# Sixteen early score tiles: mask and maximum as products on TensorE, the exponential in the fetch

## The chip, the core and the metric

The kernel runs on one core of one Trainium2 chip. The core has five engines that run on their own and wait for each other by semaphores: TensorE (PE in the trace, with its weight loads as PEld), VectorE (DVE), ScalarE (ACT), GpSimd (POOL) and SyncE (SP, which issues most DMAs). The metric is the device time of one execution in microseconds.

## The reference, cut to what matters

The program computes attention in which every row keeps only its 32 largest scores, and then feeds the result to a mixture of experts. There are 8 batches of 8 heads, 576 positions, and 64 values per head; the experts are 8 of 512 x 1024 and 1024 x 512.

```python
scores = scale * np.matmul(q, k.transpose(0, 1, 3, 2))
kth = np.partition(scores, -top_k, axis=-1)[..., -top_k:-top_k + 1]
scores = np.where(scores >= kth, scores, -1000000000.0)
attn = np.exp(scores - np.max(scores, axis=-1, keepdims=True))
attn = attn / (np.sum(attn, axis=-1, keepdims=True) + 1e-09)
x = np.matmul(attn, v)            # per head; then (4608, 512)
...
e_idx = np.argmax(x @ w_gate + modality_bias[modality_id], axis=1)
for e in range(E):
    h = np.maximum(x[mask] @ w1[e], 0.0)
    out[mask] = gate_w[mask, None] * (h @ w2[e])
```

## The kernel before

Scores are worked on in tiles of 128 rows by 576 columns. Two heads form a pair and have 9 tiles: eight full ones, four to a head, and one that joins the last 64 rows of both. There are 32 pairs and 288 tiles. `role(i)` is the place of tile `i` in its pair; roles 0 to 7 are the full tiles in couples (the two heads of one row block), role 8 is the joint one.

The schedule is written by hand. One pass of the main loop, a step, issues one piece of work for each of some ten tiles in different states; the engines then run their own queues in exactly that order. In step `i` the tiles are these:

- tile i+2: scores on TensorE (`qk`), copied to SBUF by ScalarE as `Ssb` (`sevac`)
- tiles i and i-1, VectorE: the maxima of six column blocks (`subs`, tile `cand`), and from them the 24 largest of a row (`chain`, tile `mg`, three maxima at L407 to L409). The third of these maxima releases `n` on GpSimd (`below`, L421), which holds the 24th largest
- tile i-3, ScalarE: `sign`, which marks and counts the scores not above that bound (tile `K`); tile i-4, GpSimd: `pool_y`, the product `y` of scores and marks (L434); tile i-5, VectorE: `find`, the next eight of a row from `y` (L438)
- in every third step three small VectorE instructions for three tiles at once, `pick` (`eq`, `jk`, `kth`, L445 to L447), which choose the 32nd largest of a row, `kth`, and on GpSimd `small` (`sm`, L415), the negated row maxima
- tile i-7, at the end of VectorE's step: the masking, in one of two forms. The usual form is `keep` (L458): ScalarE has already taken the exponential (`expo`, tile `ex`), and one VectorE instruction compares, multiplies and sums the row into `den`. GpSimd then runs a tiny `gate` (`spare`, L481) that waits for `keep`, ahead of the next `y`. The other form is for early tiles, those below tile 48 whose number is not 2 modulo 3: VectorE writes only the mask as a large negative number (`hide`, L465, tile `hT`, lent from the experts), GpSimd adds it to the scores one step later (`hidden`, L471, tile `ex`), and ScalarE takes the exponential with the row's sum (`masked`, L477, tile `P`)
- tile i-9: TensorE transposes `P` in blocks of 128 columns (`trans`), ScalarE copies the result to `PT` (`evac`), and the products with v follow (`av`)

VectorE's order inside a step comes from `arrange`, which places the pieces by a table of costs and earliest starts. The order on GpSimd is that of the calls: `hidden`, then `gate`, `pool_y`, in one step of nine two copies `qbd` (`fill`), then `below` and `small`.

Experts start when the first batch of four pairs has been routed. From then on each step also gets expert work for TensorE from a budget fixed in the program. Until then idle steps carry filler products with ones (`keep_warm`, L973). At the end, `bounds` and `beyond` check that the thresholds lay in a safe range; otherwise the program repeats the work in a slow form (`slow`).

Of the kernel before, what the change touches and what calls it, by code (L numbers as in the profile page):

```python
# [42 lines left out]
LR = LT + 2  # L43
# [13 lines left out]
QO = 0  # L57
# [20 lines left out]
def kernel(  # L78
# [274 lines left out]

    st0 = wk.tile([128, 2, 2, S], FR, name="ks", bufs=2)
    role = lambda i: (i - 1) % 9

    def unstacked(j):

# [26 lines left out]
        T[i] = {"ps": ps[:, :, :288]}  # L385

    def sevac(i):
        T[i]["S"] = sb = wk.tile([128, S], FT, name="Ssb", bufs=LR + 1 + QL - QO)
        A.activation(sb.rearrange("p (a b) -> p a b", a=2), T[i]["ps"], AF.Copy, scale=0.125)  # L389

    bnd = [(x * S) // NSUB for x in range(NSUB + 1)]
# [17 lines left out]
                lambda: V.max(m[:, 16:24], c3)]  # L409

    def small(i0):
        s = wk.tile([128, 3], FT, name="sm", bufs=6)
        for x in range(3):
            T[i0 + x]["s"] = s
        G.tensor_scalar(s, T[i0]["mg"][:, :, 0], -1.0, 1.0, op0=OP.mult, op1=OP.mult)  # L415

    def below(i):
        t = T[i]
# [68 lines left out]

    def trans(i):
        c, h = divmod(role(i), 2)
        T[i]["pt"] = psT.tile([128, 5, 128], FT, name="T")  # L490
        for x in range(4 if c < 4 and h == 0 else 5):
            PE.transpose(T[i]["pt"][:, x, :], (Pm if c == 4 else Pb[c % 2])[:, h * 512 + x * 128:h * 512 + x * 128 + 128], idf)  # L492

    def evac(i):
        c, h = divmod(role(i), 2)
        if c < 4:
            o, n = PT[:, c, 4 * h:4 + 5 * h], 4 + h
        else:
            o, n = PT[:, 1, 4:], 5
        A.activation(o, T[i]["pt"][:, :n], AF.Copy)  # L500

    def av(p, j, x):

# [469 lines left out]
            PE.matmul(ps[:, :256].rearrange("p (a b) -> p a b", a=2), onesb, onesb[:, None, :].to_broadcast([128, 2, 128]), start=True, stop=True)  # L973

    keep_warm(KW)
    bd_ = const.tile([128, 4], FT, name="bad")
    badi = const.tile([1, 1], I32, name="badi")

    def bounds():

        bt = wk.tile([128, S], BF, name="K", bufs=KB).bitcast(FT)[:, :NT]
        V.tensor_scalar(bt, kth, KTH_MIN, 0.0, op0=OP.is_le, op1=OP.add, accum_out=bd_[:, 0:1])
        V.tensor_scalar(bt, kth, KTH_MAX, 0.0, op0=OP.is_ge, op1=OP.add, accum_out=bd_[:, 1:2])

    def beyond():

        bb = bd_.bitcast(BF)[:, 4:6]
        V.tensor_scalar(bb, bd_[:, 0:2], 0.0, None, op0=OP.is_gt)
        pbad = psX.tile([128, 2], FT, name="X")
        PE.matmul(pbad, onesb, bb, start=True, stop=True)  # L990
        V.tensor_reduce(bd_[:, 3:4], pbad, axis=AX.X, op=OP.add)
        V.tensor_copy(badi, bd_[0:1, 3:4])
# [130 lines left out]
    for i in range(LAST):  # L1123
# [104 lines left out]
        if ok(u) and role(u) in (3, 7, 8):  # L1228
# [261 lines left out]
```

## Time and profile before

| what | value |
|---|---|
| time, median of 3 runs (lowest to highest) | 1192.18 us (1190.52 to 1195.83) |
| the profiled execution, its own time | 1191.36 us |
| its span (first to last instruction) | 1189.7 us |
| busy share of the span: PE, DVE, ACT, POOL | 97%, 92%, 83%, 56% |
| granted clock of TensorE, mean | 0.995 |
| first tile's `find` on VectorE | 18.6 us |
| first expert product's weights (w1b) requested | 173.97 us |

The span is the part of the time that the trace shows; what lies around it is 1.7 us here. A busy share counts every moment in which an instruction of the engine is under way; VectorE's instructions overlap at their ends, so their durations add up to more than the busy time, and the distance from one start to the next is the better measure of what one costs. TensorE's busy share before 170 us holds the fillers. The last 190 us have little attention work, and TensorE is the engine with the most to do there.

### The profile page before, as it was taken

How to read it: one execution, taken by the hardware profiler on the slowest of the kernel's cores; microseconds unless marked ns; L12 is line 12 of the kernel's file. 1: busy time of each engine (PE TensorE's matmuls, PEld its weight loads, DVE VectorE, ACT ScalarE, POOL GpSimd, SP SyncE). 2: the span in 40 equal slices, each digit the busy share in tenths (PEclk: the TensorE clock that was granted, in tenths of full speed). 3: DMA queues.
4: the chain of work that ended last, by engine and by line, in shares of the span. 5: the costliest groups of instructions: out<-in, count | busy, mean ns of one | idle time of the engine just before them, and what ended most of it. 6: DMA issues, size and time to landing. Idle time of an engine off the chain costs nothing.

```text
span 1189.7 us, 28032 instructions
## 1 busy us (share of the span) xinstructions
PE 1150.4 (97%) x7902; PEld 904.1 (76%) x7902; DVE 1089.2 (92%) x5474; ACT 981.5 (83%) x2015; POOL 670.6 (56%) x1256
## 2 busy tenths in 40 slices
PE   8889979999999999999999999999999999999998
PEld 6667768777777868777686877778687777589987
DVE  7999999999999999999999899999999999476762
ACT  5999979998889979998999899989999887355653
POOL 6888875555656565566566566557655665221111
PEclk9999999999999999999999999999999999999999
DMA  5663357653677368654785448664765554287750
GB/s 125 161 183 90 89 164 221 191 151 87 169 221 199 86 178 241 170 151 129 199 244 156 129 134 242 168 163 133 204 185 134 173 145 148 71 288 250 245 191 22
DMA packets 204323, 197.09 MB, mean 166 GB/s; under 512 B 104413, under 2 KB 151533, under 8 KB 204160
## 3 DMA queue, kind: packets, MB, share of 16 engines
q1 hardware_dynamic: 196880, 175.92, 53.4%
q0 software_dynamic: 6080, 19.00, 4.4%
q8 instruction: 66, 1.08, 0.4%
q14 instruction: 97, 0.79, 0.2%
q10 hardware_dynamic: 1200, 0.30, 0.1%
HBM read 118.63 MB, written 24.23 MB: 120 GB/s over the span
## 4 chain that ended last, share of the span: by engine, by line
PE 64%; DVE 23%; ACT 6%; issue 2%; DMA 2%; POOL 1%; SPq 0%; POOLq 0%; ACTq 0%; DVEq 0%
PE E L798 11%; PE E L811 11%; PE X L520 10%; PE S L384 8%; PE T L492 7%; DVE cand L396 6%; PE X L1085 5%; PE X L1069 4%; DVE mg L438 4%; DVE P L458 4%; PE E L1069 1%; PE X L318 1%; ACT K L428 1%; ACT Ssb L389 1%; DVE cand L407 1%
## 5 line engine op out<-in xcount | busy, mean ns | idle before, releaser
L396 DVE MAX8 cand<-Ssb 128x8 f32<-128x96 f32 x1728 | 389.5, 245 | 2.1 <-ACT Ssb L389 2.1
L434 POOL TENSOR_TENSOR y<-Ssb,K 128x576 f32<-128x576 f32 x288 | 368.2, 1279 | 8.9 <-ACT K L428 8.6
L428 ACT ACTIVATE K<-Ssb,n 128x576 bf16<-128x576 f32 x288 | 230.0, 799 | 9.2 <-POOL y L434 9.0
L384 PE MATMUL S<-ks,qs 128*128 128x288 f32 x992 | 222.7, 346 | 9.9 <-ACT Ssb L389 6.5
L389 ACT ACTIVATE Ssb<-S 128x576 f32<-128x576 f32 x284 | 187.9, 662 | 53.5 <-PE S L384 32.4
L438 DVE MAX8 mg<-y 128x8 f32<-128x576 f32 x288 | 213.4, 741 | 3.9 <-POOL y L434 3.9
L798 PE MATMUL E<-xgT,w1b 128*128 128x256 f32 x832 | 201.2, 384 | 3.5 <-ACT hT L802 1.6
L452 ACT ACTIVATE ex<-Ssb,sm 128x576 f32<-128x576 f32 x256 | 202.9, 793 | 0.0
L500 ACT ACTIVATE PT<-T 128x640 f32<-128x640 f32 (+1 forms) x288 | 193.6, 672 | 6.7 <-PE T L492 6.6
L811 PE MATMUL E<-w2b,hT 128*128 128x512 f32 x416 | 195.8, 597 | 0.5 <-ACT hT L802 0.2
L384 PEld LDWEIGHTS S<-ks,qs 128*128 128x128 f32 x992 | 152.9, 190 | 56.8 <-issue 26.0
L458 DVE SCALAR_TENSOR_TENSOR P<-Ssb,kth,ex 128x576 f32<-128x576 f32 x230 | 191.3, 832 | 3.0 <-ACT ex L452 1.7
L492 PE MATMUL T<-idf,P 128*128 128x128 f32 x1152 | 169.6, 274 | 6.3 <-ACT P L477 5.3
L798 PEld LDWEIGHTS E<-xgT,w1b 128*128 128x128 f32 x832 | 150.8, 190 | 30.0 <-ACT hT L802 6.6
L481 POOL TENSOR_SCALAR spare<-P 1x1 f32<-1x1 f32 x230 | 41.9, 182 | 211.7 <-DVE mg L407 175.0
L492 PEld LDWEIGHTS T<-idf,P 128*128 128x128 f32 x1152 | 137.6, 141 | 12.5 <-ACT P L477 8.8
L520 PE MATMUL X<-PT,vm 128*64 128x256 f32 (+1 forms) x1536 | 145.2, 331 | 1.0 <-ACT xgT L757 0.5
L520 PEld LDWEIGHTS X<-PT,vm 128*64 128x64 f32 x1536 | 87.7, 137 | 45.3 <-issue 10.7
L421 POOL TENSOR_SCALAR n<-mg 128x1 f32<-128x1 f32 x288 | 67.5, 234 | 96.4 <-DVE mg L409 78.9
L811 PEld LDWEIGHTS E<-w2b,hT 128*128 128x128 f32 x416 | 72.6, 190 | 59.6 <-issue 54.7
L428 ACT ACTIVATION_READ_ACCUMULATOR K<-Ssb,n 128x1 f32 x288 | 64.0, 222 | 0.0
L1091 POOL DMA_INDIRECT out_dram<-ot,tk x12 | 12.3, 1026 | 91.0 <-ACT ot L1090 91.0
(223 smaller groups left out, 2146.5 us busy)
## 6 DMA issues: line engine op xcount, KB each, us to landing
w1b<-in_moe_w_dram SPq DMA_DIRECT2D x76, 512.0 KB
w2b<-in_moe_w_dram SPq DMA_DIRECT2D x76, 512.0 KB
ks<-st SPq DMA_DIRECT2D x62, 288.0 KB
ks<-st SPq DMA_DIRECT2D x62, 256.0 KB
qs<-st SPq DMA_DIRECT2D x124, 128.0 KB
xg<-xs SPq DMA_DIRECT2D x19, 516.0 KB
vm<-in_v_dram SPq DMA_DIRECT2D x32, 256.0 KB
km<-in_k_dram SPq DMA_DIRECT2D x63, 128.0 KB
```

The costliest lines, as they stand in the source:

```text
L384: PE.matmul(ps[:, hf, :288], l, m, start=(n == 0), stop=(n == len(terms) - 1))
L389: A.activation(sb.rearrange("p (a b) -> p a b", a=2), T[i]["ps"], AF.Copy, scale=0.125)
L396: return [lambda s=s: V.max(c[:, s * 8:s * 8 + 8], T[i]["S"][:, bnd[s]:bnd[s + 1]]) for s in range(NSUB)]
L428: A.activation(t["K"], t["S"], AF.Sign, scale=2.0 ** -24 - 1.0, bias=t["n"][:, 1, i % 3:i % 3 + 1], accum_out=t["n"][:, 0, i % 3:i % 3 + 1])
L434: G.tensor_tensor(t["y"], t["S"], t["K"], op=OP.mult)
L438: V.max(t["mg"][:, i % 3, 24:32], t["y"])
L452: A.activation(t["ex"], t["S"], AF.Exp, bias=t["s"][:, i % 3:i % 3 + 1])
L458: V.scalar_tensor_tensor(t["P"], t["S"], kth[:, i:i + 1], t["ex"], op0=OP.is_ge, op1=OP.mult, accum_out=dn)
L492: PE.transpose(T[i]["pt"][:, x, :], (Pm if c == 4 else Pb[c % 2])[:, h * 512 + x * 128:h * 512 + x * 128 + 128], idf)
L520: PE.matmul(o.rearrange("p (a b) -> p a b", a=2) if j < 8 else o, l, r, start=(c == 0), stop=(c == 4))
L798: PE.matmul(ps[:, f % 2], w1b[:, c, f * 128:(f + 1) * 128], xgT[:, c, :], start=(c == 0), stop=(c == KC - 1))
L811: PE.matmul(o["py"], hT[:, f, t * 128:(t + 1) * 128], w2b[:, f, :], start=(f == 0), stop=(f == FC - 1))
```

## The change

Sixteen tiles, those of roles 0 to 3 among the first 36 (`wide`), take a new path. Their scores are copied not into `Ssb` but into parts of the expert weight buffers `w1b` and `w2b`, which are not yet in use (`swide`). At the end of its step VectorE writes a mask of 1 or a tiny number as bf16 (`hide_wide`, in place of `hide`). GpSimd's addition falls away for them. ScalarE makes a diagonal matrix from the row's negated maximum (`top_wide`, tile `dg`). TensorE transposes the scores themselves and adds, by one or two bf16 products for each block, the mask times the diagonal (`trans_wide`), so that PSUM holds the transposed scores less the maximum, and far below zero where masked. The fetch by ScalarE takes the exponential in place of the copy (`evac`). The sums of rows come from products of ones with `PT`, once for each pair (`sums_wide`), with a copy, two tiny products and a second copy.

The other twenty tiles among the first 36 are all early now, including those of number 2 modulo 3, which had `keep`, `expo` and `gate`. In five steps for each of the four pairs the fillers fall away (`quiet`). The negated maxima of the first 36 tiles are kept in `tops` and checked at the end.

```diff
+WIDE = 36
+BIG = float(2.0 ** 80)
+    swide = [flat(t)[:, n * 2 * S:(n + 1) * 2 * S] for t, n in ((w1b, 0), (w1b, 1), (w1b, 2), (w2b, 0))]
+    hwide = [flat(t)[:, o:o + 640].bitcast(BF) for t, o in ((xgT, 0), (hT, 1024))]
+    G.memset(sel[:, 0:1, :], 1.0)
+    G.memset(sel[:, 1:3, :], 0.0)
+    for x in range(2):
+        G.memset(sel[x * 64:x * 64 + 64, 1 + x, :], 1.0)
+        G.memset(hwide[x][:, S:S + 128], 0.0)
+    V.tensor_scalar(idw, idf, BIG * (1.0 + 2.0 ** -7), None, op0=OP.mult)
...
+    wide = lambda i: main[0] and i < WIDE and role(i) < 4
...
     def sevac(i):
-        T[i]["S"] = sb = wk.tile([128, S], FT, name="Ssb", bufs=LR + 1 + QL - QO)
+        if wide(i):
+            n, _, h = wide_of(i)
+            sb = swide[n][:, h * S:h * S + S]
...
+    def hide_wide(i):
+        V.tensor_scalar(hwide[b][:, h * (S + 128):h * (S + 128) + S], T[i]["S"], kth[:, i:i + 1], 1.0 / BIG,
+                        op0=OP.is_lt, op1=OP.max)
+    def top_wide(i):
+        A.activation(t["dg"], idw, AF.Copy, scale=t["s"][:, i % 3:i % 3 + 1])
+    def trans_wide(i):
+        for x in range(4 + h):
+            PE.matmul(pt[:, x, :], swide[n][:, a:a + 128], idf, start=(x % 4 == 0), stop=False,
+                      is_transpose=True, skip_group_check=True)
+            for m, (o, u) in enumerate(cut):
+                PE.matmul(pt[:, x, :], hb[:, o:o + 128], T[u]["dg"], start=False, stop=(m == len(cut) - 1),
+                          skip_group_check=True)
+    def sums_wide(p):
+            for c in range(c0, c1):
+                for h in range(2):
+                    PE.matmul(st["po"][h * 64:h * 64 + 64, :256].rearrange("p (a b) -> p a b", a=2),
+                              sel[:, 0 if c < 4 else 1 + h, :], PT[:, 0:2, c + 5 * h if c < 4 else 4, :],
+                              start=(c == 0), stop=(c == 4), skip_group_check=True)
+                xev.append(lambda: A.activation(stage, st["po"][:, :256], AF.Copy))
...
-        A.activation(o, T[i]["pt"][:, :n], AF.Copy)
+        A.activation(o, T[i]["pt"][:, :n], AF.Exp if wide(i) else AF.Copy)
...
-    early = lambda u: u < EARLY and u % 3 != 2
+    early = lambda u: u < WIDE or u < EARLY and u % 3 != 2
...
         if ok(i - 1 - LR) and early(i - 1 - LR):
-            hidden(i - 1 - LR)
+            if not wide(i - 1 - LR):
+                hidden(i - 1 - LR)
...
-            masked(u, dn_of(u))
+            top_wide(u) if wide(u) else masked(u, dn_of(u))
...
+            if role(u) == 3 and wide(u):
+                avs.extend(sums_wide(u // 9))
+                quiet[0] = i + 4
-        if not seen[0] and FILL <= i < NT:
+        if not seen[0] and quiet[0] < i < NT:
             keep_warm(NW)
...
-            end.append(Op("keep", lambda: hide(u) if early(u) else keep(u, dn_of(u)), got, *cut_))
+            end.append(Op("keep", lambda: hide_wide(u) if wide(u) else hide(u) if early(u) else keep(u, dn_of(u)), got, *cut_))
```

What GpSimd's queue holds in steps 9 to 12 (tiles 1 to 3 and the next to be masked) is, before, with `ex` for the addition, `y` for the product, `n` for the 24th largest, `sm` for the maxima and `spare` for the gate:

```order
L471 TENSOR_TENSOR ex<-Ssb,hT 128x576
L434 TENSOR_TENSOR y<-Ssb,K 128x576
L421 TENSOR_SCALAR n<-mg 128x1
L481 TENSOR_SCALAR spare<-P_119 1x1
L434 TENSOR_TENSOR y<-Ssb,K 128x576
L421 TENSOR_SCALAR n<-mg 128x1
L415 TENSOR_SCALAR sm<-mg 128x3
L471 TENSOR_TENSOR ex<-Ssb,hT 128x576
L434 TENSOR_TENSOR y<-Ssb,K 128x576
L421 TENSOR_SCALAR n<-mg 128x1
```

and in the changed kernel, on the same engine at the same place (`tops` holds the maxima):

```order
L462 TENSOR_TENSOR y<-Ssb,K 128x576
L449 TENSOR_SCALAR n<-mg 128x1
L462 TENSOR_TENSOR y<-Ssb,K 128x576
L449 TENSOR_SCALAR n<-mg 128x1
L443 TENSOR_SCALAR tops<-mg 128x3
L462 TENSOR_TENSOR y<-Ssb,K 128x576
L449 TENSOR_SCALAR n<-mg 128x1
L462 TENSOR_TENSOR y<-Ssb,K 128x576
L449 TENSOR_SCALAR n<-mg 128x1
L499 TENSOR_TENSOR ex<-Ssb,hT 128x576
```

The instruction that waited for VectorE's masking, `ex` or `spare`, is gone from in front of each `y`; it is back with the last row, for tile 5.

Two steps later on GpSimd, steps 15 and 16, whose tiles 7 and 8 stay on the old path, stood before:

```order
L471 TENSOR_TENSOR ex<-Ssb,hT 128x576
L434 TENSOR_TENSOR y<-Ssb,K 128x576
L421 TENSOR_SCALAR n<-mg 128x1
L481 TENSOR_SCALAR spare<-P_120 1x1
L434 TENSOR_TENSOR y<-Ssb,K 128x576
L421 TENSOR_SCALAR n<-mg 128x1
L415 TENSOR_SCALAR sm<-mg 128x3
```

and now stands there:

```order
L499 TENSOR_TENSOR ex<-Ssb,hT 128x576
L462 TENSOR_TENSOR y<-w1b,K 128x576
L449 TENSOR_SCALAR n<-mg 128x1
L499 TENSOR_TENSOR ex<-Ssb,hT 128x576
L462 TENSOR_TENSOR y<-w2b,K 128x576
L449 TENSOR_SCALAR n<-mg 128x1
L443 TENSOR_SCALAR tops<-mg 128x3
```

In the step that has `pick` on VectorE, the one with the maxima as its last row, an `ex` stands in front of `y` where the small `spare` stood.

VectorE itself at the end of step 9 and the start of step 10 had, before, behind the third maximum of `chain`:

```order
L409 MAX mg<-cand_692 128x8
L396 MAX cand<-Ssb 128x8 x3
L458 SCALAR_TENSOR_TENSOR P_119,den_125<-Ssb,kth,ex 128x576
L407 MAX mg<-cand 128x8
L438 MAX mg<-y 128x8
```

and has now:

```order
L436 MAX mg<-cand_690 128x8
L423 MAX cand<-Ssb 128x8 x3
L504 TENSOR_SCALAR xgT<-w1b,kth 128x576
L434 MAX mg<-cand 128x8
L466 MAX mg<-y 128x8
```

Only the masking instruction is another; the places of the maxima and of `pick` are the same in all these steps.

## Rows read from the trace of the kernel before

**Rows 1.** Busy time by windows: first and last of four groups of nine steps.

```profile
core 0: us, PE busy (x) PEld busy (x) DVE busy (x) ACT busy (x) POOL busy (x), PEclk, DMA share, GB/s
29.99:57.82 27.83, 24.00 (x186) 19.23 (x185) 27.83 (x149) 25.93 (x58) 23.80 (x33) 0.94 0.58 156
...
113.40:141.19 27.79, 24.87 (x205) 19.33 (x205) 27.79 (x149) 26.59 (x61) 23.83 (x33) 1.00 0.41 96
```

**Rows 2.** Timeline of VectorE, three steps: start us, duration us, instruction.

```profile
79.67 0.74 DVE L438 MAX8 mg<-y 128x8 f32<-128x576 f32 x1
...
81.27 0.17 DVE L445 TENSOR_TENSOR eq<-i9s,n 128x27 f32<-128x27 f32 x1
81.36 0.20 DVE L409 MAX8 mg<-cand 128x8 f32<-128x48 f32 x1
...
82.14 0.50 DVE L465 TENSOR_SCALAR hT<-Ssb,kth 128x576 bf16<-128x576 f32 x1
...
82.68 0.74 DVE L438 MAX8 mg<-y 128x8 f32<-128x576 f32 x1
...
84.28 0.19 DVE L409 MAX8 mg<-cand 128x8 f32<-128x48 f32 x1
...
84.87 0.69 DVE L465 TENSOR_SCALAR hT<-Ssb,kth 128x576 bf16<-128x576 f32 x1
...
85.60 0.74 DVE L438 MAX8 mg<-y 128x8 f32<-128x576 f32 x1
...
87.80 1.05 DVE L458 SCALAR_TENSOR_TENSOR P<-Ssb,kth,ex 128x576 f32<-128x576 f32 x1
...
88.91 0.74 DVE L438 MAX8 mg<-y 128x8 f32<-128x576 f32 x1
```

**Rows 3.** Timeline of GpSimd, the same steps; in brackets idle time and its end.

```profile
81.65 0.22 POOL L421 TENSOR_SCALAR n<-mg 128x1 f32<-128x1 f32 x1 [0.47 <-DVE mg L409]
81.92 0.20 POOL L415 TENSOR_SCALAR sm<-mg 128x3 f32<-128x3 f32 x1
82.72 1.28 POOL L471 TENSOR_TENSOR ex<-Ssb,hT 128x576 f32<-128x576 f32 x1 [0.60 <-DVE hT L465]
83.97 1.28 POOL L434 TENSOR_TENSOR y<-Ssb,K 128x576 f32<-128x576 f32 x1
85.33 0.28 POOL L421 TENSOR_SCALAR n<-mg 128x1 f32<-128x1 f32 x1
85.71 1.28 POOL L471 TENSOR_TENSOR ex<-Ssb,hT 128x576 f32<-128x576 f32 x1
...
89.01 0.18 POOL L481 TENSOR_SCALAR spare<-P 1x1 f32<-1x1 f32 x1
89.16 1.28 POOL L434 TENSOR_TENSOR y<-Ssb,K 128x576 f32<-128x576 f32 x1
```

**Rows 4.** Timelines of GpSimd and of VectorE at 300 us.

```profile
299.88 1.27 POOL L434 TENSOR_TENSOR y<-Ssb,K 128x576 f32<-128x576 f32 x1
...
300.10 1.10 DVE L445 TENSOR_TENSOR eq<-i9s,n 128x27 f32<-128x27 f32 x1
```

**Rows 5.** Timelines at two places where both engines start within 0.03 us.

```profile
72.89 0.20 POOL L415 TENSOR_SCALAR sm<-mg 128x3 f32<-128x3 f32 x1
...
72.92 0.50 DVE L465 TENSOR_SCALAR hT<-Ssb,kth 128x576 bf16<-128x576 f32 x1
...
196.84 0.85 POOL L415 TENSOR_SCALAR sm<-mg 128x3 f32<-128x3 f32 x1
...
196.83 0.80 DVE L458 SCALAR_TENSOR_TENSOR P<-Ssb,kth,ex 128x576 f32<-128x576 f32 x1
```

**Rows 6.** Groups by line, 20 to 140 us: count, busy us, mean ns, idle before.

```profile
L477 ACT ACTIVATE P<-ex,sm 128x576 f32<-128x576 f32 x20 | 16.2, 811 | 0.0
...
L291 ACT ACTIVATE st<-X 128x128 fp32r<-128x128 f32 x4 | 1.1, 276 | 0.0
...
L973 PE MATMUL E<-onesb 128*128 128x256 bf16 x246 | 34.0, 275 | 0.1
```

**Rows 7.** Timeline of GpSimd at the start: the first `qbd`, idle time in brackets.

```profile
6.58 0.29 POOL L346 TENSOR_SCALAR qbd<-ks 64x128 fp32r<-64x128 f32 x1 [0.81 <-DVE ks L293]
```

More of the change, by code (lines that the diff above doesn't have):

```diff
@@ L37 @@
 KW = 10
-FILL = 0
 KP = 2
@@ L70 @@
 EARLY = 48
+WIDE = 36
+BIG = float(2.0 ** 80)
+MAX_TOP = 64.0
 EPS = 1e-9
@@ L230 @@
     mbt = const.tile([128, 2, E], FT, name="mbt")
+    flat = lambda t: t.rearrange("p a b -> p (a b)")
+    swide = [flat(t)[:, n * 2 * S:(n + 1) * 2 * S] for t, n in ((w1b, 0), (w1b, 1), (w1b, 2), (w2b, 0))]
+    sel = flat(w2b)[:, 2 * S:2 * S + 192].rearrange("p (x d) -> p x d", x=3)
+    stage = flat(w2b)[:, 2 * S + 192:2 * S + 448]
+    hwide = [flat(t)[:, o:o + 640].bitcast(BF) for t, o in ((xgT, 0), (hT, 1024))]
[4 more added lines that the diff above has]
+        G.memset(hwide[x][:, S:S + 128], 0.0)
+    idw = const.tile([128, 128], BF, name="idw")
+    V.tensor_scalar(idw, idf, BIG * (1.0 + 2.0 ** -7), None, op0=OP.mult)
+    tops = const.tile([128, WIDE], FT, name="tops")
+    main = [True]
     zr = const.tile([128, XW], FT, name="zr")
@@ L355, with wide_of @@
     role = lambda i: (i - 1) % 9
+    wide = lambda i: main[0] and i < WIDE and role(i) < 4
+    def wide_of(i):
+        c, h = divmod(role(i), 2)
+        return (i // 9 * 2 + c) % 4, c % 2, h
     def unstacked(j):
@@ L387, in sevac @@
     def sevac(i):
-        T[i]["S"] = sb = wk.tile([128, S], FT, name="Ssb", bufs=LR + 1 + QL - QO)
+        if wide(i):
+            n, _, h = wide_of(i)
+            sb = swide[n][:, h * S:h * S + S]
+        else:
+            sb = wk.tile([128, S], FT, name="Ssb", bufs=LR + 1 + QL - QO)
+        T[i]["S"] = sb
         A.activation(sb.rearrange("p (a b) -> p a b", a=2), T[i]["ps"], AF.Copy, scale=0.125)
@@ L411, in small @@
     def small(i0):
-        s = wk.tile([128, 3], FT, name="sm", bufs=6)
+        on = main[0] and i0 < WIDE
+        s = tops[:, i0:i0 + 3] if main[0] and i0 < WIDE else wk.tile([128, 3], FT, name="sm", bufs=6)
         for x in range(3):
             T[i0 + x]["s"] = s
-        G.tensor_scalar(s, T[i0]["mg"][:, :, 0], -1.0, 1.0, op0=OP.mult, op1=OP.mult)
+        G.tensor_scalar(s, T[i0]["mg"][:, :, 0], -1.0, 0.0 if on else 1.0, op0=OP.mult, op1=OP.min if on else OP.mult)
     def below(i):
@@ L471, in hidden, with part, rows @@
         G.tensor_tensor(t["z"], t["S"], t["hb"], op=OP.add)
+    def hide_wide(i):
+        _, b, h = wide_of(i)
+        V.tensor_scalar(hwide[b][:, h * (S + 128):h * (S + 128) + S], T[i]["S"], kth[:, i:i + 1], 1.0 / BIG,
+                        op0=OP.is_lt, op1=OP.max)
+    def top_wide(i):
+        t = T[i]
+        t["dg"] = wk.tile([128, 128], BF, name="dg", bufs=3)
+        A.activation(t["dg"], idw, AF.Copy, scale=t["s"][:, i % 3:i % 3 + 1])
+    def trans_wide(i):
+        n, b, h = wide_of(i)
+        hb = hwide[b]
+        T[i]["pt"] = pt = psT.tile([128, 5, 128], FT, name="T")
+        for x in range(4 + h):
+            a = h * 512 + x * 128
+            PE.matmul(pt[:, x, :], swide[n][:, a:a + 128], idf, start=(x % 4 == 0), stop=False,
+                      is_transpose=True, skip_group_check=True)
+            cut = [(x * 128, i)] if not h else [(512, i - 1), (640, i)] if x == 0 else [(640 + x * 128, i)]
+            for m, (o, u) in enumerate(cut):
+                PE.matmul(pt[:, x, :], hb[:, o:o + 128], T[u]["dg"], start=False, stop=(m == len(cut) - 1),
+                          skip_group_check=True)
+    def sums_wide(p):
+        st = {}
+        def part(c0, c1):
+            if c0 == 0:
+                st["po"] = psE.tile([128, 260], FT, name="E")
+            for c in range(c0, c1):
[3 more added lines that the diff above has]
+                              start=(c == 0), stop=(c == 4), skip_group_check=True)
+            if c1 == 5:
+                xev.append(lambda: A.activation(stage, st["po"][:, :256], AF.Copy))
+        def rows():
+            for c in range(2):
+                PE.matmul(st["po"][:, 256 + 2 * c:258 + 2 * c], stage[:, c * 128:c * 128 + 128], idf[:, 0:128:64],
+                          start=(c == 0), stop=(c == 1), skip_group_check=True)
+            xev.append(lambda: A.activation(den[p // HP % 2][:, p % HP, 0:4], st["po"][:, 256:260], AF.Copy))
+        return [(1.5, lambda: part(0, 3)), (1.0, lambda: part(3, 5)), (0.2, rows)]
     def masked(i, dn):
@@ L489, in trans @@
         c, h = divmod(role(i), 2)
+        if wide(i):
+            trans_wide(i)
+            return
         T[i]["pt"] = psT.tile([128, 5, 128], FT, name="T")
@@ L975 @@
     keep_warm(KW)
-    bd_ = const.tile([128, 4], FT, name="bad")
+    bd_ = const.tile([128, 6], FT, name="bad")
     badi = const.tile([1, 1], I32, name="badi")
@@ L983, in bounds @@
         V.tensor_scalar(bt, kth, KTH_MAX, 0.0, op0=OP.is_ge, op1=OP.add, accum_out=bd_[:, 1:2])
+        V.tensor_scalar(bt[:, :WIDE], tops, -MAX_TOP, 0.0, op0=OP.is_le, op1=OP.add, accum_out=bd_[:, 2:3])
     def beyond():
-        bb = bd_.bitcast(BF)[:, 4:6]
-        V.tensor_scalar(bb, bd_[:, 0:2], 0.0, None, op0=OP.is_gt)
-        pbad = psX.tile([128, 2], FT, name="X")
+        bb = bd_.bitcast(BF)[:, 8:11]
+        V.tensor_scalar(bb, bd_[:, 0:3], 0.0, None, op0=OP.is_gt)
+        pbad = psX.tile([128, 3], FT, name="X")
         PE.matmul(pbad, onesb, bb, start=True, stop=True)
@@ L1016 @@
     turn = [0]
+    quiet = [-1]
     def acc(shape):
@@ L1379 @@
     slot(SURE)
-    bad = nc.values_load(badi[:, :], min_val=0, max_val=256)
-    more = nc.values_load(morei[:, :], min_val=0, max_val=N + 256)
+    bad = nc.values_load(badi[:, :], min_val=0, max_val=384)
+    more = nc.values_load(morei[:, :], min_val=0, max_val=N + 384)
     slot(None)
@@ L1407, in slow @@
     def slow():
+        main[0] = False
         Pb[:] = [wk.tile([128, 2 * S], FT, name=f"P{i}", bufs=1) for i in range(2)]
```

## The prediction

> **What bounds the kernel now.** I read the windows first, then two timelines side by side. A program step handles one score tile and is bounded in the trace by two successive `find` maxima (L438). Nine steps belong to a pair of heads; the change concerns the steps from 29.99 us to 141.19 us, which are four such groups. Each takes 27.8 us, VectorE has no idle time in them, ScalarE is busy about 26 us and TensorE 24 to 25 us, of which part is filler [rows 1]. In the first group the granted clock is 0.94 on the mean and the nine steps are no longer for it, so TensorE does not set the pace. VectorE does.
>
> Three steps show how [rows 2]. From 79.67 to 82.68 is 3.01 us (this step also picks the 32nd largest: `eq`, `jk`, `kth`), from 82.68 to 85.60 is 2.92, from 85.60 to 88.91 is 3.31 (it ends with the product L458). The reader is to compare these with GpSimd [rows 3]. In the first, `hide` (L465) starts at 82.14 with GpSimd idle until 82.72 and takes 0.50. In the second it starts at 84.87, `y` runs until 83.97 + 1.28 = 85.25, and `hide` takes 0.69. In the third L458 starts at 87.80 under the next `y` and takes 1.05. So VectorE instructions of these kinds wait for a running GpSimd sum or product. The clearest row: a tiny `eq` that takes 0.17 at 81.27 takes 1.10 at 300.10, because `y` had started at 299.88 and ends at 301.15 [rows 2, 4]. A maximum of 48 columns takes 0.20 without `y` (81.36) and 0.19 under it (84.28) [rows 2], so these don't wait. The kernel before dodges these waits: after each L458 comes a `spare` on GpSimd that waits for it, then `y` (89.01, 89.16) [rows 3], and in the pick step `y` is over before `eq` starts, since that tile has no `ex` sum ahead of it.
>
> **The change part by part.** *VectorE.* Every third tile loses L458 for a `hide`: twelve tiles. Free of waits a step without pick is 2.19 (82.68 to 84.87) plus 0.54 (82.14 to 82.68) = 2.73, one with pick 3.01. Nine free steps are 6 x 2.73 + 3 x 3.01 = 25.4 against 27.8 now. This is all that can be gained: 2.4 us per group, 9.6 in four. The new mask has the shape of the old `hide`, so the same price.
>
> *GpSimd.* The wide tiles lose the `ex` sum, the others of every third place get one, all `spare` rows go. In sum it is less work, but its order against VectorE is what counts, in three places.
>
> First, wide steps without pick. With no `ex` to wait for, `y` starts straight behind `n`. `n` starts 0.09 after the third maximum ends (81.36 + 0.20, 81.65), and the next instruction 0.27 behind it (81.92) [rows 2, 3]. So `y` starts 0.19 + 0.09 + 0.27 = 0.55 after that maximum started, and `hide` 0.59 after it (84.28, 84.87): `y` leads by 0.04. If it takes precedence it runs from 2.15 to 3.43 of the step, and the next `find` comes 0.35 after its end (85.25 to 85.60), at 3.78 instead of 2.73: 1.05 lost. The other way costs nothing. As to which: at 72.92 a `hide` starts 0.03 behind `sm`, and `sm` keeps its 0.20; at 196.84 `sm` starts 0.01 behind L458 and is held for 0.85 [rows 5]. Hence I take precedence for `y`. The order shows it in three wide steps of each group, one of them with a pick. There `sm` sits between `n` and `y`, so `y` starts about 0.82 after the maximum, `hide` 0.78 after it (81.36 to 82.14): `hide` leads and nothing is lost. Two collisions: 2.1 us a group.
>
> The Trainium skill (SBUF — State Buffer, "SBUF: two separate sides") says VectorE and GpSimd share a port pair under an exclusive lock, taken for a whole instruction by whoever starts first. The 1.10 agrees. If instead the pair were shared by halves, as the 0.69 alone might suggest, the two collisions would cost about 0.3 each and the forecast would be some 6 us lower by them.
>
> Second, pick steps of the tiles that stay with `ex`. Before, these steps had no `ex` in front of `y`. Now they have: `ex` starts 0.04 into the step (82.72), `y` 1.25 later (83.97) and ends 2.57 into it [rows 3], while `eq` is due at 1.60. By 300.10 the loss is the remaining time less 0.12 (1.05 left, 0.93 longer): 0.85. In the second such step of a group GpSimd runs 0.11 late (`ex` at 85.71 against `find` at 85.60), so 0.92. Together 1.8 us a group.
>
> Third, the other steps with `ex`: `hide` waits for the end of `y` as at 84.87, 2.92 to 2.99 instead of 2.73, three steps, 0.7 us a group. The step after the last wide one is free, since `ex` there waits for `hide`.
>
> Sum of a group: 25.4 + 2.1 + 1.8 + 0.7 = 30.0, against 27.8: 2.2 slower, four groups 8.7 us.
>
> *ScalarE.* 24 masked exponentials with their accumulator reads and 12 plain ones become 20 masked ones, 16 diagonals of 128 columns and eight small copies: 16 fewer of 0.81, 16 more of 0.28 [rows 6], so about 7 us less. The fetch turns from copy to exponential at equal shape; even 0.1 us more for each of 16 would be 1.6. VectorE hides all of it; I take nothing for it. Without that cover ScalarE, at 26 of 27.8 us, would only be eased.
>
> *TensorE.* 80 mask products of 128 columns and 40 products with ones over 256 columns come; 120 fillers of 256 columns go, 34.0/246 = 0.14 us each [rows 6]. No product is wider than a filler, so the work stays even; were the 40, in float32, to take twice a filler, it would be 5.6 us more over four groups. Its cover is TensorE's idle time, 3 us a group, and the fillers that stay; without it each microsecond would count.
>
> *The rest.* Six small memsets come ahead of `qbd` on GpSimd, about 0.7 us by their neighbours' sizes; GpSimd idles 0.81 before `qbd` now [rows 7], so nothing, and at worst some tenths. The check of the maxima adds one instruction of 36 columns and a third column: 0.2 us, not counted. The expert buffers lent to the tiles are read last some steps before the first weight load in the program's order, so no load waits.
>
> The profiled execution took 1191.36 us, 1.7 more than its span. 1191.36 + 8.7 = 1200.1; it lies 0.8 below the median of the runs, 1192.18, so for a median I forecast 1200.9 us. TensorE is full from some 190 us on and the work per step there is fixed, so a shift early is a shift at the end.
>
> **The rivals.** *All `hide` win.* A lead of 0.04 us is little. Then the 2.1 a group goes: 27.9 a group, 1192.5 us, no change. For it speaks that the start stamps are of two engines and that a small lead was decisive only in rows of other instructions. The Trainium skill (Perfetto Trace Analysis, "GPSIMD Engine Instruction") calls the spans of this engine unreliable and its start stamp the moment of its first read; no row here shows how far that holds for a `y` 0.04 ahead.
>
> *`y` wins in the wide pick step too.* Its lead there is -0.03 us, and the gap behind `sm` is taken from that behind `n`. It would end at 2.51 + 1.28 = 3.79 and the step last 4.14 instead of 3.01: 1.13 a group more, 1205.4 us. This is the dearer rival on the slow side.
>
> *`eq` isn't held and all `hide` win*, because GpSimd's queue falls into another alignment. Then only the 0.7 remains: 26.1 a group, 1.7 less than now, 1185.4 us. It needs the row at 300.10 not to repeat. This one is faster.
>
> *TensorE late.* Five steps per pair lose their fillers; if the clock fell to its lower level there and score products came late by about 1 us a group, 1205. The 0.94 of the first group, without longer steps, speaks against it [rows 1].
>
> *The change doesn't act*: the maxima check sends the kernel into its slow repeat. With the inputs' small scores I give it nothing.
>
> **How the numbers follow.** Forecast 0.46, no collisions lost or only one in two 0.28 (1192.5, or 1196.7 for half), all lost 0.14, `eq` free 0.06, TensorE late 0.06. The range holds the first three with a little beyond: 1191 to 1206. A difference of 0.5%, about 6 us, is what a measurement of this kernel can tell from no change. Slower by more than that: the forecast, save a few hundredths where its sum runs short, with the dear rival and the late TensorE, 0.6. Within: 0.35, most of it from the second case. Faster: 0.05, from the free `eq`.
>
> **What would show it.** In the changed kernel's timeline: pick steps with `ex` near 3.9 us, with an `eq` of 0.9 to 1.1; wide steps without pick near 3.8 with a `hide` of 1.4 to 1.6, or 2.73 with `hide` 0.5 and `y` held; groups of nine steps near 30.0 us; ScalarE with more idle time and no effect. It is wrong if `eq` stays at 0.2 us, if VectorE shows idle time in the first 150 us, or if the time from 200 us to the end differs from before by more than a microsecond or two.

## The result and the profile after

The changed kernel takes 1207.46 us (median of 4 runs, 1206.91 to 1208.25) against 1193.74 us for the kernel before (4 runs). The ratio is 1.0122 with a 95% interval of 1.0103 to 1.0142: it is slower by 1.2%, some 14 us (the medians differ by 13.7). The forecast was 1200.9, and 1206 the end of its range. The direction was right, the size was not.

The profiled execution took 1208.25 us (span 1206.6), 16.9 us more than the one before. The windows of the four groups of nine steps, from `find` to `find` (now L466), answer to [rows 1]:

```profile
core 0: us, PE busy (x) PEld busy (x) DVE busy (x) ACT busy (x) POOL busy (x), PEclk, DMA share, GB/s
29.79:61.04 31.25, 26.43 (x215) 20.85 (x214) 31.25 (x145) 26.90 (x62) 21.28 (x29) 0.94 0.67 175
61.04:92.31 31.27, 27.93 (x224) 21.33 (x222) 31.27 (x145) 26.06 (x62) 21.29 (x29) 0.92 0.54 148
92.31:123.59 31.28, 26.99 (x222) 20.70 (x219) 31.28 (x145) 26.07 (x62) 21.31 (x29) 0.95 0.39 90
123.59:154.82 31.23, 27.74 (x216) 20.65 (x213) 31.23 (x145) 25.89 (x61) 21.21 (x29) 0.89 0.37 85
```

VectorE is still without idle time, with three or four instructions fewer in a group, and a group lasts 31.26 us, where the forecast had 30.0. ScalarE has more slack than before, about 5 of 31 us, since the group is longer, and it gains nothing. Where the time goes is seen in VectorE's timeline of the second group (start, duration; only `find`, `eq` and the masks L504 and L493), which answers to [rows 2]:

```profile
61.04 0.73 DVE L466 MAX8 mg<-y 128x8 f32<-128x576 f32 x1
...
63.23 1.55 DVE L504 TENSOR_SCALAR xgT<-w1b,kth 128x576 bf16<-128x576 f32 x1
...
64.83 0.74 DVE L466 MAX8 mg<-y 128x8 f32<-128x576 f32 x1
...
67.32 1.55 DVE L504 TENSOR_SCALAR hT<-w2b,kth 128x576 bf16<-128x576 f32 x1
...
68.92 0.73 DVE L466 MAX8 mg<-y 128x8 f32<-128x576 f32 x1
...
71.11 1.56 DVE L504 TENSOR_SCALAR hT<-w2b,kth 128x576 bf16<-128x576 f32 x1
...
72.71 0.73 DVE L466 MAX8 mg<-y 128x8 f32<-128x576 f32 x1
...
74.90 0.49 DVE L493 TENSOR_SCALAR hT<-Ssb,kth 128x576 bf16<-128x576 f32 x1
...
75.44 0.73 DVE L466 MAX8 mg<-y 128x8 f32<-128x576 f32 x1
...
77.05 1.00 DVE L473 TENSOR_TENSOR eq<-i9s,n 128x27 f32<-128x27 f32 x1
...
79.30 0.74 DVE L466 MAX8 mg<-y 128x8 f32<-128x576 f32 x1
...
81.48 0.92 DVE L493 TENSOR_SCALAR hT<-Ssb,kth 128x576 bf16<-128x576 f32 x1
```

and in GpSimd's of the same stretch, which answers to [rows 3]:

```profile
63.19 1.28 POOL L462 TENSOR_TENSOR y<-Ssb,K 128x576 f32<-128x576 f32 x1
...
66.80 0.22 POOL L449 TENSOR_SCALAR n<-mg 128x1 f32<-128x1 f32 x1 [2.33 <-DVE mg L436]
67.08 0.24 POOL L443 TENSOR_SCALAR tops<-mg 128x3 f32<-128x3 f32 x1
67.28 1.28 POOL L462 TENSOR_TENSOR y<-Ssb,K 128x576 f32<-128x576 f32 x1
...
71.07 1.28 POOL L462 TENSOR_TENSOR y<-Ssb,K 128x576 f32<-128x576 f32 x1
...
76.72 1.28 POOL L462 TENSOR_TENSOR y<-Ssb,K 128x576 f32<-128x576 f32 x1
...
80.81 1.28 POOL L462 TENSOR_TENSOR y<-w1b,K 128x576 f32<-128x576 f32 x1
```

The masks of all three wide steps take some 1.55 us, not of two: each time `y` starts 0.04 ahead of the mask (63.19 and 63.23, 67.28 and 67.32, 71.07 and 71.11), and the mask ends some 0.3 after `y`. The steps last 3.79, 4.09 and 3.79 us. The step after them is free (2.73). `eq` at 77.05 waits for the `y` of 76.72: 1.00 us, step 3.86. The second such `eq` of the group takes 1.05 and its step 3.90.

A second loss comes once, ahead of the first routing. The waits of VectorE from 20 to 200 us now hold a row that the kernel before does not have:

```profile
DVE lt L661 <- PE X L653: 2.1, 1, 2.1
```

That step (`lt` is an instruction of the routing, which picks the experts from products of TensorE) lasts from 164.38 to 171.53, 7.15 us; its like before lasted 4.99. Some 10 us ahead of this wait TensorE's granted clock is at 0.57 and 0.58 on the mean, and 16 of the products with v take 3.68 us:

```profile
154.00:158.00 4.00, 3.52 (x16) 2.43 (x18) 4.00 (x17) 3.81 (x9) 3.71 (x5) 0.57 0.02 6
158.00:162.00 4.00, 4.00 (x21) 2.15 (x18) 4.00 (x24) 1.58 (x6) 2.47 (x6) 0.58 0.00 0
```

```profile
156.79 3.68 PE L599 MATMUL X<-PT,vm 128*64 128x256 f32 x16
```

The same products in the kernel before:

```profile
142.48 1.95 PE L520 MATMUL X<-PT,vm 128*64 128x256 f32 x16
```

The account of the 16.9 us: -0.2 up to the first group (29.79 against 29.99), 13.8 in the four groups (125.03 against 111.20), 2.2 in the step of the routing, and 1.1 in the other 1000 us, nearly all of it in two steps of the changed kernel, at 648 and at 671 us (4.13 for 3.47 and 3.73 for 3.32). From 200 us on the distance between the kernels changes by 0.9, as forecast.

### The profile page after: what moved, and what is told of

It reads as the page before. It is cut to its first block, busy times and chain, and to the rows that moved or that the text cites. A ratio compares the mean times of both kernels' runs of the same rounds, so it can differ in the third digit from the quotient of the medians.

```text
span 1206.6 us, 28091 instructions
## 1 busy us (share of the span) xinstructions
PE 1162.4 (96%) x7958; PEld 910.3 (75%) x7958; DVE 1104.3 (92%) x5465; ACT 979.6 (81%) x2019; POOL 660.6 (55%) x1246
## 3 DMA queue, kind: packets, MB, share of 16 engines
q8 instruction: 66, 1.08, 0.4%
## 4 chain that ended last, share of the span: by engine, by line
PE 51%; DVE 39%; ACT 5%; issue 2%; POOL 1%; DMA 1%; SPq 0%; POOLq 0%; ACTq 0%; DVEq 0%
DVE cand L423 10%; PE E L877 9%; PE E L890 8%; PE X L599 8%; DVE mg L466 7%; PE S L406 6%; PE T L571 5%; DVE P L486 5%; PE X L1166 5%; PE X L1150 4%; DVE cand L434 2%; DVE cand L435 2%; DVE mg L436 2%; PE E L1150 1%; DVE mg L434 1%
## 5 line engine op out<-in xcount | busy, mean ns | idle before, releaser
L423 DVE MAX8 cand<-Ssb 128x8 f32<-128x96 f32 x1632 | 367.2, 244 | 1.2 <-ACT Ssb L416 1.2
L462 POOL TENSOR_TENSOR y<-Ssb,K 128x576 f32<-128x576 f32 x272 | 347.7, 1278 | 10.5 <-ACT K L456 9.2
L456 ACT ACTIVATE K<-Ssb,n 128x576 bf16<-128x576 f32 x272 | 216.2, 795 | 11.4 <-POOL y L462 11.2
L416 ACT ACTIVATE Ssb<-S 128x576 f32<-128x576 f32 x270 | 177.9, 659 | 49.3 <-PE S L406 33.5
L466 DVE MAX8 mg<-y 128x8 f32<-128x576 f32 x288 | 213.2, 740 | 3.9 <-POOL y L462 3.9
L480 ACT ACTIVATE ex<-Ssb,sm 128x576 f32<-128x576 f32 x244 | 193.2, 792 | 0.0
L486 DVE SCALAR_TENSOR_TENSOR P<-Ssb,kth,ex 128x576 f32<-128x576 f32 x218 | 178.6, 819 | 3.2 <-ACT ex L480 1.7
L571 PE MATMUL T<-idf,P 128*128 128x128 f32 x1080 | 158.8, 274 | 7.5 <-ACT P L553 6.5
L571 PEld LDWEIGHTS T<-idf,P 128*128 128x128 f32 x1080 | 129.0, 141 | 13.8 <-ACT P L553 10.2
L449 POOL TENSOR_SCALAR n<-mg 128x1 f32<-128x1 f32 x288 | 63.6, 221 | 122.1 <-DVE mg L436 105.5
L456 ACT ACTIVATION_READ_ACCUMULATOR K<-Ssb,n 128x1 f32 x272 | 59.4, 218 | 0.0
```

The costliest lines, as they stand in the source:

```text
L423: return [lambda s=s: V.max(c[:, s * 8:s * 8 + 8], T[i]["S"][:, bnd[s]:bnd[s + 1]]) for s in range(NSUB)]
L456: A.activation(t["K"], t["S"], AF.Sign, scale=2.0 ** -24 - 1.0, bias=t["n"][:, 1, i % 3:i % 3 + 1], accum_out=t["n"][:, 0, i % 3:i % 3 + 1])
L462: G.tensor_tensor(t["y"], t["S"], t["K"], op=OP.mult)
L466: V.max(t["mg"][:, i % 3, 24:32], t["y"])
L480: A.activation(t["ex"], t["S"], AF.Exp, bias=t["s"][:, i % 3:i % 3 + 1])
```

## The experiments

Ratios are against the kernel before on the same chip, with 95% intervals. The first four start from the changed kernel and undo or move one thing each.

**A gate behind the wide masks.**

```diff
+    def gate_wide(i):
+        _, b, h = wide_of(i)
+        o = h * (S + 128) // 2
+        G.tensor_scalar(spare[:, 0:1], hwide[b].bitcast(FT)[0:1, o:o + 1], 1.0, 1.0, op0=OP.mult, op1=OP.mult)
...
         if ok(i - 1 - LR) and not early(i - 1 - LR):
             gate(i - 1 - LR)
+        if ok(i - 1 - LR) and wide(i - 1 - LR):
+            gate_wide(i - 1 - LR)
```

> The changed kernel with one tiny GpSimd instruction per wide tile that reads the mask and so holds y until VectorE has written it. Theory (y and the mask collide; whoever starts first keeps the other waiting): the masks of the three wide steps take 0.5 us in place of 1.55, the steps fall from 3.79, 4.09, 3.79 to about 2.75, 3.05, 2.75, a group of nine steps from 31.27 to about 28.1, all four groups by 12.8 us; ratio to the kernel before near 1.001. Rival (the new mask costs 1.55 by itself, by its form or its place in memory): masks stay at 1.55, ratio 1.012. Second rival (the held y makes find late): steps lengthen elsewhere, VectorE idle, ratio above 1.005.

Measured: 1195.87 us, 1.0027 (1.0015 to 1.0038). VectorE's masks and GpSimd's gates in the second group:

```profile
59.95 0.50 DVE L504 TENSOR_SCALAR xgT<-w1b,kth 128x576 bf16<-128x576 f32 x1
...
62.98 0.52 DVE L504 TENSOR_SCALAR hT<-w2b,kth 128x576 bf16<-128x576 f32 x1
...
65.73 0.50 DVE L504 TENSOR_SCALAR hT<-w2b,kth 128x576 bf16<-128x576 f32 x1
```

```profile
60.60 0.18 POOL L563 TENSOR_SCALAR spare<-xgT 1x1 f32<-1x1 f32 x1 [0.77 <-DVE mg L434]
60.75 1.27 POOL L462 TENSOR_TENSOR y<-Ssb,K 128x576 f32<-128x576 f32 x1
```

The steps are 2.73, 3.05 and 2.73, a group 28.1 (the last 28.5). The mask itself costs 0.5; all the rest of its 1.55 was waiting, 3.2 us a group. The routing's wait is still there (1.5 us), hence 1.0027 and not 1.001.

**`y` moved by a tenth of a microsecond.**

```diff
+    def tiny():
+        G.tensor_scalar(spare[:, 0:1], zr[0:1, 0:1], 1.0, 1.0, op0=OP.mult, op1=OP.mult)
...
+        if ok(i - 1 - LR) and wide(i - 1 - LR):
+            tiny()
```

> The changed kernel with one tiny GpSimd instruction ahead of y in the steps after wide tiles that waits for nothing; it only moves the start of y by 0.15 to 0.2 us, from 0.04 ahead of the mask to 0.1 or more behind it. Theory (the earlier start takes precedence): masks 0.5 us, steps near 2.75, 3.05, 2.75, ratio near 1.001, and y starts late or takes about 0.4 longer. Rival (GpSimd's product goes first even when it starts a little later): masks stay near 1.6 to 1.7, steps near 3.95 and 4.25, ratio 1.013 to 1.015.

Measured: 1198.91 us, 1.0052 (1.0032 to 1.0072). In seven of the eight wide steps without pick of the four groups, `y` now starts 0.10 or 0.11 behind the mask, the mask takes 0.49 or 0.50 and `y` is held (1.53 or 1.54); in the eighth `y` starts 0.71 behind. Of the four wide pick steps three still lose, though `y` starts 0.10 or 0.11 behind there too; in the fourth, where it starts 0.30 behind, the mask takes 0.49. The pick step and the wide step after it, in the second group:

```profile
62.99 1.70 DVE L504 TENSOR_SCALAR hT<-w2b,kth 128x576 bf16<-128x576 f32 x1
...
66.92 0.49 DVE L504 TENSOR_SCALAR hT<-w2b,kth 128x576 bf16<-128x576 f32 x1
```

```profile
63.09 1.27 POOL L462 TENSOR_TENSOR y<-Ssb,K 128x576 f32<-128x576 f32 x1
...
67.03 1.54 POOL L462 TENSOR_TENSOR y<-Ssb,K 128x576 f32<-128x576 f32 x1
```

So neither theory holds as written. At 0.10 behind, all three steps with pick lose and all seven without pick win; the stamps do not tell the two kinds apart, and no run shows why they differ. In three steps without pick of other runs below even 0.02 to 0.04 behind was enough for the mask (62.44 in the run with the fillers put back: mask 0.49, `y` held to 1.63). With two tiny instructions in a row `y` starts later still:

> The changed kernel with two wait-free tiny instructions in place of one, so that y would start about 0.25 us behind the mask. With one of them, y 0.10 behind, the mask of the three later wide pick steps still waited (1.70 us). Theory (only the order of the two requests counts, and 0.10 us is about the gap between a start stamp and a request): all masks take 0.5 us, pick steps 3.05, groups near 28.1, ratio 1.001 to 1.004. Rival (in a pick step VectorE waits for whatever GpSimd runs back to back from sm on): masks of the wide pick steps stay above 1.6, groups 29.3 or more, ratio 1.005 or more.

Measured: 1194.78 us, 1.0021 (1.0003 to 1.0039). The masks of the wide steps take 0.49 to 0.52, also those with pick, and the groups last 28.1. The wide pick step of the second group:

```profile
63.10 0.52 DVE L504 TENSOR_SCALAR hT<-w2b,kth 128x576 bf16<-128x576 f32 x1
```

```profile
63.06 0.60 POOL L562 TENSOR_SCALAR spare<-zr 1x1 f32<-1x1 f32 x2
63.63 1.28 POOL L462 TENSOR_TENSOR y<-Ssb,K 128x576 f32<-128x576 f32 x1
```

`y` starts 0.51 to 0.53 behind the mask in all wide steps, just as the mask ends, and not 0.25 as expected: the two tiny instructions themselves take 0.60 here, where they take 0.45 with no mask beside them (57.95). With `y` clearly behind, a pick step loses nothing either, so the rival is refuted; why the pick steps lose at 0.10 stays open. The routing does not wait in this run, nor in the one before it.

**The tiles of number 2 modulo 3 put back.**

```diff
-    early = lambda u: u < WIDE or u < EARLY and u % 3 != 2
+    early = lambda u: wide(u) or u < EARLY and u % 3 != 2
```

> The changed kernel with the twelve tiles of number 2 modulo 3 that aren't wide put back to the old masking with the gate; the wide path stays. Theory (eq waits under y because an ex stands ahead of it): eq back to 0.17 us, the two pick steps from 3.85 and 3.90 to 3.09 and 3.01, the steps before them 3.04 and 3.28 for their STT (before: 2.73 and 2.97), group 31.27 to about 29.95, 5.3 us in all; ratio near 1.0077. Rival (eq is late for its own input from ScalarE, whose queue has changed): eq stays near 1.0, ratio 1.012 or more.

Measured: 1201.50 us, 1.0077 (1.0053 to 1.0101), a group 29.86. The two pick steps that had lost, in the second group:

```profile
75.86 0.16 DVE L473 TENSOR_TENSOR eq<-i9s,n 128x27 f32<-128x27 f32 x1
...
85.09 0.16 DVE L473 TENSOR_TENSOR eq<-i9s,n 128x27 f32<-128x27 f32 x1
```

`eq` is back at 0.16 with the new path in place, so it was the `ex` ahead of `y` that held it.

**All of the first 36 tiles early, without the wide path**, from the kernel before:

```diff
-    early = lambda u: u < EARLY and u % 3 != 2
+    early = lambda u: u < 36 or u < EARLY and u % 3 != 2
```

> The kernel before with nothing changed but that all of the first 36 tiles take the two-part masking; no wide path. Theory (an ex ahead of y makes every eq wait): three pick steps of a group near 3.9 with eq about 1.0, six others near 2.97, a group 29.5 against 27.8, 6.8 us in all, ratio 1.0055. Rival (eq waits in the changed kernel because of the wide tiles' order): eq stays 0.17 and a group takes 26.9, ratio 0.997.

Measured: 1202.97 us, 1.0091 (1.0071 to 1.0111). A group is 29.8, with three pick steps of 3.9 and `eq` at 1.04 to 1.08, each under a `y` that has an `ex` ahead of it:

```profile
53.62 1.05 DVE L445 TENSOR_TENSOR eq<-i9s,n 128x27 f32<-128x27 f32 x1
```

```profile
53.35 1.28 POOL L434 TENSOR_TENSOR y<-Ssb,K 128x576 f32<-128x576 f32 x1
```

The mechanism is as expected and 0.3 a group dearer. The rest of the excess, 3.2 us, appears in its profile only in VectorE's steps from 590 us on, and starts at TensorE: near 581 us it is idle for 2.63 us until a DMA brings the tokens of an expert (`xg`), where it waits 0.53 us for them in the kernel before, and from 584 to 588 us its granted clock is at 0.61 on the mean. Why the tokens come later there is not shown.

**The fillers put back** in the changed kernel, into unused columns of the tile of the sums:

```diff
-        if not seen[0] and quiet[0] < i < NT:
-            keep_warm(NW)
+        if not seen[0] and i < NT:
+            keep_warm(NW) if quiet[0] < i else warm_beside(NW)
```

> The changed kernel with the fillers of the twenty quiet steps put back, into unused columns of the tile of the row sums. Theory (without them TensorE's clock falls to its lower level, the products with v before the first routing take 3.7 us in place of 1.95, and VectorE waits for them once for 2.07 us near 165 us): clock 1.0 in all windows from 56 to 160 us, no such wait, 2.2 us less; ratio near 1.0103. Rival (the routing is late for another reason): the wait stays, ratio 1.012. Second rival (the fillers themselves make TensorE late): more waits for TensorE before 165 us, ratio above 1.012.

Measured: 1208.72 us, 1.0132 (1.0106 to 1.0158): no gain. The clock is 1.0 from 40 to 104 us, but it falls again late, and VectorE waits 2.2 us for the routing as before. TensorE from 136 us on:

```profile
138.16 0.80 PE L406 MATMUL S<-ks,qs 128*128 128x288 f32 x4 [2.31 <-ACT Ssb L416]
...
140.56 3.68 PE L598 MATMUL X<-PT,vm 128*64 128x256 f32 x16
...
156.62 1.95 PE L598 MATMUL X<-PT,vm 128*64 128x256 f32 x16
```

and ScalarE ahead of it:

```profile
137.46 0.65 ACT L416 ACTIVATE Ssb<-S 128x576 f32<-128x576 f32 x1 [2.44 <-POOL ex L499]
```

TensorE had worked off its queue during the long wide steps and stood idle for 2.31 us: it waited for ScalarE's copy, this for a score buffer, this for GpSimd's `ex`, and `ex` for VectorE's mask. Behind that idle time the clock was at its lower level (0.50 from 140 to 144 us, 1.2 GHz). So fillers alone do not keep the clock up while the steps stay long. But from 146 us on it was at 1.00 again, and the products right ahead of the routing (156.62) took 1.95 us. They started 3.7 us into their step, where the kernel before has them 1.3 us into it. What keeps the routing waiting here is thus a TensorE that is late at full clock, as in the second rival; how much of that comes from the slow stretch and how much from the fillers is not shown. With the routing done this run is 1.8 us ahead of the changed kernel, because some wide masks went ahead of `y` (0.49 at 39.76 and at 62.44); by the end it has lost that again.

**The fillers taken away** from the kernel before, in the same twenty steps:

```diff
-        if not seen[0] and FILL <= i < NT:
+        if not seen[0] and not (14 <= i < 50 and i % 9 in (5, 6, 7, 8, 0)) and FILL <= i < NT:
```

> The kernel before, with nothing changed but that the fillers of the same twenty steps fall away. Theory (the lost fillers alone let TensorE's clock fall, and the products before the first routing come late): granted clock below 1 in some windows from 56 to 150 us, up to 2 us of VectorE waiting for the routing's products near 150 us, ratio 1.001 to 1.002. Rival (it takes the long steps of the changed kernel too, in which TensorE waits for VectorE's buffers): clock 1.0 up to 150 us, no such wait, ratio 1.000.

Measured: 1196.66 us, 1.0028 (1.0013 to 1.0043). Two windows of it, and VectorE's steps behind them:

```profile
112.00:120.00 8.00, 5.94 (x29) 4.33 (x29) 8.00 (x45) 7.93 (x20) 6.62 (x10) 0.72 0.12 37
120.00:128.00 8.00, 7.83 (x72) 5.98 (x69) 7.87 (x44) 4.97 (x12) 6.08 (x7) 0.85 0.00 0
```

```profile
128.77 1.43 DVE L465 TENSOR_SCALAR hT<-Ssb,kth 128x576 bf16<-128x576 f32 x1
...
134.11 0.76 DVE L438 MAX8 mg<-y 128x8 f32<-128x576 f32 x1 [1.06 <-POOL y L434]
...
136.32 1.25 DVE L458 SCALAR_TENSOR_TENSOR P<-Ssb,kth,ex 128x576 f32<-128x576 f32 x1
```

The clock falls where fillers are gone (0.72 and 0.85; 1.00 in the kernel before), with nothing else changed. The price comes at another place than expected: the routing is on time here, but near 126 us TensorE is late, `y` waits 2.0 us for `K`, runs into the masks (1.43, 1.25) and keeps `find` waiting (1.06). By the routing the kernel is 2.4 us behind. Again some 3 us more appear in steps from 590 us on. TensorE there, first in the kernel before and then in this run:

```profile
575.37 0.66 PE L783 MATMUL X<-idf,xg 128*128 128x128 f32 x4 [0.53 <-DMA xg<-xs]
...
579.39 0.78 PE L783 MATMUL X<-idf,xg 128*128 128x128 f32 x4 [2.36 <-DMA xg<-xs]
```

It waits longer for the tokens, its clock is at 0.60 on the mean from 580 to 584 us (1.00 in the kernel before), and the steps that lengthen follow. That the one causes the other is read from their order, not shown by a run.

**Both cures together**, gate and tiles put back; then also all fillers; then a third of them:

```diff
+            keep_warm(NW) if quiet[0] < i else warm_beside(1)
```

> The changed kernel with both cures: the gate behind wide masks, and the twelve tiles of number 2 modulo 3 on their old path. Theory (the loss is these collisions and nothing else, so their cures add): steps 2.73, 3.01, 2.73, 3.04, 3.01, 2.92, 3.29, 3.01, 2.92, a group 26.7 against 27.8 before; 4.5 us faster than the kernel before, ratio 0.996, or 0.998 if the first routing still waits 2 us for TensorE. Rival (the wide path costs something that the collisions hid, such as late transposes or a late expert load): ratio 1.000 or above, with VectorE idle in the first 150 us.

> As the run with both cures, and the fillers of the quiet steps put back. Theory (with even steps the fillers hold the clock up): clock 1.0 from 56 to 150 us, first routing without wait, ratio 0.996. Rival (fillers don't matter, the clock falls where TensorE waits for VectorE): the same time and the same waits as without them.

> Both cures, and in the quiet steps a third of the fillers (two products in place of six). Theory (without fillers the clock falls once near 110 us and three steps there lose 2.3 us; with all of them TensorE has no slack, a late y in step 13 of each group costs 0.8 us and the routing 1.3 us): some fillers avoid most of both, groups near 26.8, less than 1 us lost to late y or to the routing, ratio 0.996 to 0.998. Rival (no amount between helps): clock falls as without fillers, or y is late as with all, ratio 0.998 to 1.000.

Measured: with no fillers 1190.10 us, 0.9983 (0.9973 to 0.9993); with all 1191.05 us, 0.9994 (0.9983 to 1.0004); with a third **1188.70 us, 0.9967 (0.9953 to 0.9981)**, 0.3% faster than the kernel before. The cures add: without fillers the first three groups last 26.8 us, as worked out. What is left is TensorE. Without fillers the last group's clock falls to 0.88 on the mean and three steps lose 1.8 us to a late `y`. With all fillers the clock is 1.00 from 56 to 150 us, but TensorE is busy 47.91 of 48 us from 56 to 104, groups last 27.3 to 27.6 (in one step of each `y` starts 0.7 to 1 us late, and `eq` takes 0.74 to 1.04), and the routing waits 1.3 us, with no low clock ahead of it. With a third, windows of the second to the fourth group:

```profile
57.70:84.53 26.83, 25.27 (x230) 20.22 (x231) 26.83 (x148) 25.61 (x62) 20.12 (x33) 1.00 0.72 199
84.53:111.25 26.72, 25.07 (x229) 19.99 (x229) 26.72 (x148) 24.89 (x58) 19.98 (x33) 1.00 0.56 135
111.25:138.05 26.80, 25.74 (x229) 20.12 (x229) 26.80 (x148) 25.60 (x61) 19.71 (x33) 1.00 0.44 100
```

The clock stays up, TensorE has 1.1 to 1.7 us of slack in a group, the routing is on time, and these groups are 1.0 us shorter than those of [rows 1]; the first still takes 27.8, with a late `y` in one step.

## Why the prediction was right and wrong

**VectorE as the bound: right.** No idle time in the four groups, every step as long as its VectorE instructions and their waits.

**Wide steps without pick: right.** 3.78 forecast, 3.79 measured, by the mechanism named; the gate shows that the price is the wait.

**The wide pick step: wrong, and the largest miss.** Forecast 3.01, measured 4.09 in every group: 1.08 x 4 = 4.3 us. The forecast's median of 1200.9 with this alone put right would be 1205.2. The step that failed is the start of `y` behind `sm`. I took 0.27 us for the distance from `sm` to `y`, which is the distance from `n` to `sm`. It is 0.20 (67.08 to 67.28, with `tops` in place of `sm`), and the mask starts 0.80 after the maximum (66.52 to 67.32), not 0.78, so that `y` leads by 0.04 where I had the mask lead by 0.04. The rival "`y` wins in the wide pick step too" was the truth here, at its price of 1.13. I gave it too little: a lead of 0.04 worked out of gaps between other instructions carries no sign. The run with `y` moved says more: even a lead of 0.10 by the stamps was not safe for the mask in a pick step. The Trainium skill (SBUF — State Buffer, "SBUF: two separate sides") gives the shared ports to the engine that starts first. The runs agree at 0.04 ahead and with two tiny instructions ahead of `y`; at 0.10 behind both outcomes occur, so the start stamps alone do not tell who gets the ports.

**Pick steps with `ex`: right.** Forecast 0.85 and 0.92 lost, steps near 3.9; measured 3.86 and 3.90. The run with these tiles put back returns `eq` to 0.16.

**Other steps with `ex`: short in one.** 2.97 and 2.98 as forecast, but 3.15 (79.30 to 82.45) in the step behind the first of these pick steps. That pick step has two `qbd` on GpSimd, behind its `y` (78.09, 0.67 us for both), which push `tops`, `ex` and the next `y` later, and the mask under that `y` takes 0.92. My sum left the two `qbd` out: 3.15 against 2.93, 0.22 x 4 = 0.9 us.

**TensorE: right on the groups, wrong on the routing.** I gave late TensorE 0.06, as 1 us in each group, and took [rows 1], where a clock of 0.94 cost nothing, as evidence against it. That held while only score tiles stood behind it. But ahead of the first routing VectorE waits for a chain of products, and there the low clock cost 2.2 us once. The runs without these fillers bear it out: where the 16 products ahead of the routing took 3.68 and 3.17 us (the changed kernel, the gate) the routing waited 2.1 and 1.5 us; where they took 1.95 us (one or two tiny instructions, the tiles put back, both cures, the kernel before without fillers) it did not wait. So the loss depends on where the clock happens to fall, which nothing in the forecast could give. It was also a mistake to ask the clock only of the fillers: the run with them put back shows that the long steps, too, leave TensorE idle and the clock low. And with all fillers the routing waits at full clock as well (1.3 us with both cures), so a low clock is not the only way to be late.

**ScalarE, memsets, end check: right** as nothing in the time. ScalarE's busy time in the four groups fell by 0.8 us (104.9 against 105.7), not by 7, but nothing hung on it. The start is 0.2 us earlier.

The misses add to 4.3 + 0.9 + 2.2 = 7.4. With the 8.7 forecast, the 0.2 gained at the start and the 1.1 behind the routing, for which I have no cause, that is 17.0, against 16.9 in the trace. The medians make it 13.7, since the profiled execution before was one of the quicker of its kernel (1191.36, runs from 1190.52 to 1195.83) and the one after the slowest of its four.

## What to carry to other kernels

Work taken off an engine pays only if the order that it leaves behind is as good: here each `spare` or `ex` taken from GpSimd's queue had also kept `y` off VectorE's masks. Where two engines exclude each other and a start differs by a tenth of a microsecond or less, reckon with the loss and set the order with a wait; one such instruction for each wide tile gave back 3.2 us a group. Fillers that hold a clock up are a dose: with both cures in, none cost about 2 us at one place, all took TensorE's slack, a third kept both.

## What was not expected of the hardware

- The distance from the start of one small GpSimd instruction to that of the next depends on the pair: 0.28 us from `n` to `tops`, 0.20 from `tops` to `y`, 0.15 from `spare` to `y`.
- A 128x576 mask stamped 0.10 or 0.11 us ahead of a GpSimd product waited for it in three of ten cases (1.70 us in place of 0.50), the three in pick steps.
- With both cures and a third of the fillers in the quiet steps the granted clock was 1.00 in groups two to four; with none in them, means over 8 us went down to 0.58 (the run with the gate, 112 to 120 us), and 16 products with v that take 1.95 us took up to 3.68.
